# Two chunks' projections interleaved by kind, input weights loaded earlier, and a second weight pair prepared earlier, in an attention and gated-MLP kernel

## The chip, the cores and the metric

The kernel runs on one core of one Trainium2 chip. The metric is the device time of one execution in microseconds. Below, PE is TensorE (matmuls), DVE is VectorE, ACT is ScalarE, POOL is GpSimd and SP is SyncE; SP, ACT and POOL also issue DMA transfers.

## The reference

One sequence of S = 2048 tokens with D = 1024 goes through two blocks, each behind a layer norm and with a residual. All inputs are bfloat16.

```
A (sliding dilated attention, 32 heads of 32, window 8, step 2):
  q, k, v = layernorm(x) @ wqkv
  logits[s, w] = q[s] . k[s - 2w] / sqrt(32)     (masked where s - 2w < 0)
  o[s] = sum_w softmax(logits)[s, w] * v[s - 2w]
  h = x + o @ wo
B (gated MLP with a spatial product, Fh = 1792):
  z = gelu(layernorm(h) @ w_in);  z1 = z[:, :Fh];  z2 = layernorm(z[:, Fh:])
  g = w_sp @ z2 + b_sp[:, None]
  out = h + (z1 * g) @ w_out
```

## The kernel before

**First phase: chunks of 512 tokens.** The tokens are cut into four chunks (c = 0 to 3). For each chunk there is a chain: layer norm (`ln1`), a transpose by DMA into `xnT[c]` (SP), the three projections (`qkv`: q, k and v are kinds xi = 0, 1, 2, each four accumulators of 16 matmuls with 512 columns), their copies to `stg` on ACT and stores to `qkv_d` (SP), the loads of `qT`, `kT`, `vT` of the chunk from `qkv_d` (POOL; `ld` in `attention`), the attention itself, nearly all on DVE, the output projection with the residual (`head`), and the two halves of the input projection of block B: `b_z2` (L790, with win0 and win1 of `w_in`) and `b_z1` (L856, with win2 and win3). Chunk 0 keeps q, k and v on chip.

Inside `attention` the weights of the window are spread over the partitions: half of them through PE (L617), the other half through DRAM (`spread`: one store to `att_d`, four loads into `AB`, on SP). Two sums are gathered by accumulating DMAs on POOL (`av_y<-av_z` and `av_oT<-av_zz`, L655).

**The order of the first phase** is made by a planner, the class `Order`. Every step is added with an engine, an expected duration, its dependencies, a priority and the buffers that it takes and frees. `run()` then walks through time: on the engine that can start first, it takes the step of the lowest priority number among those that can start then (a step ahead by more than 0.5 in priority is also waited for, if it can start within 0.3 of the chosen step's duration). The functions are called in the order of the planned starts, and PE, ACT, DVE and POOL keep that order, whatever the real times are. The expected durations that matter here: four projection matmuls 0.8634, a load of `qT`, `kT` or `vT` 7.0, an `xnT` transpose 9.0, a spread 7.0, a load of win0 or win1 10.0. `order()` numbers the projection matmuls 6.001, 6.002 and so on in the order in which the calls of `qkv`, `b_z2` and `b_z1` add them; `head` has priorities near 4. There are three accumulators of two banks each and four `stg` buffers. `xnT` has two buffers.

`xnT[3]` waits for three things: the normalized rows, the last use of `xnT[1]`, and the load of `vT` of chunk 1 (`G["vload", 1]`), so that the transpose stays out of the way of the sums and loads.

The weights q and k lie in two buffers with tag `wA`, v and `wo` in two with tag `wB`. win0 and win1 take over the `wA` buffers when the last q and k matmul of chunk 3 is done. Loads of large weights are kept apart by hand: `behind_spread(i_, c)` makes a DMA wait until the spread of chunk c has landed; `G["win_i", k]` remembers a load behind which the next waits.

**Second phase: the spatial product.** After `o_.run()` everything is written in the order in which it is issued. `w_sp` is read transposed, in four column blocks `raw[0]` to `raw[3]` (`load_raw`, DMA transposes on SP), scaled by powers of two per row (`scale_raw`, with `rows`, which is the turned result of `row_scales`, read back from DRAM by `rows_in`), and combined into forms (`t_forms`). Blocks 0 and 1 are the first weight pair, 2 and 3 the second. For each pair there are NQ = 7 groups of 56 matmuls (L1060) that use `zs` (forms of z2 made on DVE by `z_form`, from `z2f`, which SP loads two groups ahead), and then eight output tiles with 28 matmuls each (L1161), which end in a DVE step (L1164) and a store. During the groups of the first pair the kernel also loads the rows of `w_sp` for the second half of the row scales (`load_wn`, on ACT's queue), sums them on ACT (`row_sum`), and loads `w_out` (POOL). During the output tiles of the first pair it scales and combines the second pair (`scale_raw(2)`, `scale_raw(3)`, `t_forms(1, ...)`, `z_form(NQ, ...)`).

`bank()` hands out the eight banks of PSUM in turn; the pool behind it starts at the bank at which the accumulators of the first phase started.

Of the kernel before, what the change touches and what calls it, by code (L numbers as in the profile page):

```python
# [22 lines left out]
P = 128  # L23
NT = S // P
CH = 512
# [107 lines left out]
def kernel(  # L133
# [251 lines left out]
    def load_win(k, t):  # L385
        c0, wd = win_specs[k]
        i_ = dma_w(t[:], win_view[:, :, c0:c0 + wd])
        if k == 0:
            behind_spread(i_, 1)
        elif k < 3:  # L390
            tc.add_manual_dep(i_.ins, G["win_i", k - 1].ins.name, wait_for, reason="one load of input weights after the other")
        G["win_i", k] = i_
        wins[k] = t

    o_ = Order({"PE": 22.4, "ACT": 23.6, "DVE": 15.4, "POOL": 12.0}, {"acc": 3, "L": 1, "prod": 1, "part": 2, "xn": 4})
# [52 lines left out]
        seq[0] += 1  # L448
        return 6.0 + seq[0] * 1e-3

    def qkv(c):
        for xi in range(0 if c else 1, 3):
            wv = wsb[xi][:].rearrange("p kt (m dl) -> p kt dl m", dl=DLO)
            for dp in range(DLO // 2):
                key = ("acc", "qkv", c, xi, dp)
                deps = [G.get(("xnT", c))]
                for j, k0 in PIECES:
                    def mm(j=j, k0=k0, dl=2 * dp + j, wv=wv, key=key):
                        if j == 0 and k0 == 0:
                            G[key] = new_acc()  # L460
                        for kt in range(k0, k0 + 4):
                            T.matmul(G[key][:, j, :].rearrange("p (a b) -> p a b", a=TPC), wv[:, kt, dl, :], xnT[c][:, :, kt, :],  # L462
                                     start=(kt == 0), stop=(kt == KT - 1))
                    last = add("PE", 0.8634, mm, deps, prio=order(), take="acc" if j == 0 and k0 == 0 else None)
                    deps = [(last, 0.0)]
                def ev(xi=xi, dp=dp, key=key):
                    if c == 0:
                        A.copy(att_in[0][xi][:, 2 * dp:2 * dp + 2, HALO:HALO + CH], G[key][:])  # L468
                        if dp == 3:
                            dma(qkv_d[xi][:, :, CH - HALO:CH], att_in[0][xi][:, :, CH:CH + HALO])  # L470
                    else:
                        stg = l1.tile([P, 2, CH], BF16, name="stg", tag="xn", bufs=4)
                        A.copy(stg[:], G[key][:])  # L473
                        dma(qkv_d[xi][:, 2 * dp:2 * dp + 2, c * CH:(c + 1) * CH], stg[:])
                G["ev", c, xi, dp] = add("ACT", 0.92, ev, [last], prio=2.0, free="acc", lat=0.15, take="xn" if c else None)
                if c:
                    dma_op(3.5, lambda: None, [G["ev", c, xi, dp]], free="xn")
            G["wdone", c, xi] = last
        G["qkvlast", c] = last
# [7 lines left out]
    def attention(c):  # L487
        if c == 0:
            d_q = add("DMA", 23.7, lambda: None)
            d_k, d_v = G["ev", 0, 1, 3], G["ev", 0, 2, 3]  # L490
        else:
            def ld(which):
                def f():
                    alloc_att_in(c, which)
                    lo = c * CH - (HALO if which else 0)
                    i_ = dma_w(att_in[c][which][:], qkv_d[which][:, :, lo:(c + 1) * CH])
                    if which == 1 and c == 1:
                        behind_spread(i_, c - 1)
                    if which == 2:
                        G["vload", c] = i_  # L500
                return f
            ev = [G["ev", c, xi, dp] for xi in range(3) for dp in range(4)]
            d_q = dma_op(7.0, ld(0), ev[0:4] + [G["qfree", c - 1]] )
            d_k = dma_op(7.0, ld(1), ev[4:8] + [G["qkdone", c - 1]] + ([(G["spread", 0], 0.3)] if c == 1 else []))
            d_v = dma_op(7.0, ld(2), ev[8:12] + [G["avdone", c - 1]])
            if c == 1:
                G["xnT", 3].deps.append((d_v, 0.1))
# [458 lines left out]
        V.tensor_tensor(t[:], x, y, op=op)  # L966


    qkv(0)
    dma_op(8.0, lambda: dma_w(wo_sb[:], A_wo.rearrange("(p dl) n -> p dl n", dl=DLO)), [G["wdone", 0, 2]])  # L970
    for c in range(1, NCH):
        ln1(c)
        qkv(c)

    def open_():
        load_win(2, wtile([P, KT, 1024], "win2", "wB"))
# [8 lines left out]
    G["win", 2] = dma_op(10.0, lambda: None, [G["open"]])  # L985
    G["win", 3] = dma_op(14.0, lambda: None, [G["open"]])

    wsp_sums()
    for c in range(NCH):
        attention(c)  # L990
        if c == 1:
            G["win", 0].deps.append((G["spread", 1], 0.1))
            G["win", 1].deps.append((G["win", 0], 0.1))
            G["open"].deps.append((G["win", 1], 0.1))
        if c < NCH - 1:
            head(c)
    for c in range(NCH - 1):
# [49 lines left out]

    p2 = ctx.enter_context(tc.tile_pool(name="p2", bufs=2))
    psq = ctx.enter_context(tc.tile_pool(name="psq", bufs=8, space=PSUM))

    def bank():
        return psq.tile([P, CH], FP32, name="bank", tag="bank", bufs=8)
# [23 lines left out]
    for pr in range(NCH // 2):  # L1076
# [5 lines left out]
        for i in range(NQ):  # L1082
# [21 lines left out]
            times(k3, zs[n, 4], b22, False)  # L1104
            nc.gpsimd.tensor_tensor(p7[:], p7[:], p5[:], op=ALU.add)
            if pr == 0:
                if 2 <= i <= 5:
                    for t in (TPP + 2 * i - 4, TPP + 2 * i - 3):
                        row_sum(t, 0)
                        row_sum(t, 1)  # L1110
                if 1 <= i <= 4:
                    for t in (TPP + 2 * i - 2, TPP + 2 * i - 1):
                        load_wn(t, p2, "wn", 2)
                if i == 4:
                    dma_w(wout_a[:], wout_view[:, 0:8, :])
                elif i == 5:
                    dma_w(wout_b[:], wout_view[:, 8:NF, :])
                elif i == 6:
                    row_scales(1)
            if i + 1 < NQ:  # L1120
                for m in (3, 1, 2, 4):
                    z_form(n + 1, m)
            if n + 2 < 2 * NQ:
                for hf in range(2):
                    load_z2f(n + 2, hf)
            if pr == 0 and i >= NQ - TPC:
                load_raw(2, i - NQ + TPC, i - NQ + TPC + 1)
            V.tensor_tensor(u[:], k2[:], p1[:], op=ALU.add)
            nc.gpsimd.tensor_tensor(p1[:], u[:], bt1, op=ALU.add)
            nc.gpsimd.tensor_tensor(u[:], u[:], bt2, op=ALU.add)  # L1130
# [11 lines left out]
        for il in range(2 * TPC):  # L1142
            t = 2 * pr * TPC + il
            if pr == 0 and il == 0:
                rps = psq.tile([P, 2 * CH], BF16, name="rpq", tag="bank", bufs=8)
                T.transpose(rps[0:TPP, 0:P], rsc16[:, TPP:NT], ident[:])
                A.copy(rscT[0:TPP, :], rps[0:TPP, 0:P])
                A.dma_start(rs_d[TPP:NT, :], rscT[0:TPP, :])
                load_raw(3, 0, 1)
                load_raw(3, 1, 2)  # L1150
                rows_in(1)
                bias_in(1, p2, "z1c", 2)
                load_raw(3, 2, 3)
                load_raw(3, 3, 4)
            if il + 3 < 2 * TPC:
                load_hr(t + 3)
            hr = hrs[t]

            def project(outs, lo, hi, f):
                wt, f0 = (wout_a, f) if f < 8 else (wout_b, f - 8)  # L1160
                T.matmul(outs, zg[:, f, il * P:(il + 1) * P], wt[:, f0, lo:hi], start=(f == 0), stop=(f == NF - 1))  # L1161

            def finish_(lo, hi, acc):
                V.scalar_tensor_tensor(hr[:, lo:hi], acc[:, 0:hi - lo], rv[:, t:t + 1], hr[:, lo:hi], op0=ALU.mult, op1=ALU.add)  # L1164

            if t < NT - 1:
                acc = [bank(), bank()]
                for f in range(NF):
                    for nh in range(2):
                        project(acc[nh][:], nh * CH, (nh + 1) * CH, f)  # L1170
                for nh in range(2):
                    finish_(nh * CH, (nh + 1) * CH, acc[nh])
                dma(out2d[t * P:(t + 1) * P, :], hr[:])
            else:
                for n, (lo, hi) in enumerate(LAST_COLS):
                    acc = bank()
                    for f in range(NF):
                        project(acc[:, 0:hi - lo], lo, hi, f)
                    finish_(lo, hi, acc)
                    (A.dma_start if n % 2 else dma)(out2d[t * P:(t + 1) * P, lo:hi], hr[:, lo:hi])  # L1180
            if pr == 0:
                if il == 1:
                    scale_raw(2, 0)
                    scale_raw(2, HK)
                elif il == 3:
                    scale_raw(3, 0)
                    scale_raw(3, HK)
                elif il == 4:
                    t_forms(1, 0)
                    t_forms(1, 3)  # L1190
                elif il == 5:
                    t_forms(1, 1)
                    t_forms(1, 2)
                elif il == 6:
                    for m in (3, 1, 2, 4):
                        z_form(NQ, m)
                    bias_rows(1)
# [32 lines left out]
```

## Time and profile before

| | us |
|---|---|
| median of 3 runs (lowest to highest) | 707.87 (707.87 to 708.66) |
| the profiled execution | 711.23 |
| span of its profile | 709.2 |
| PE busy | 695.8 |
| DVE busy | 508.8 |
| ACT busy | 276.6 |
| POOL busy | 120.5 |

The span runs from the first to the last instruction of the profiled execution; its time has 2.0 us more around it. Times in rows of the trace are microseconds from the start of the span. A row of the timeline has start, duration, engine, line, operation, output and inputs, count, and in brackets how long the engine stood before it and who released it. "SPq", "ACTq" and "POOLq" are the queues in which the engines issue DMAs; the landing of a DMA is told apart from its issue. The first phase ends at about 437 us; the groups of the first weight pair run until about 523, its output tiles until about 575, the second pair's until the end.

### The profile page before, as it was taken

What the parts mean: (1) busy time and instruction counts of PE and PEld (TensorE: products, weight loads), DVE (VectorE), ACT (ScalarE), POOL (GpSimd) and SP (SyncE); (2) the same over time, 40 slices, a digit from 0 to 9 for tenths busy, and PEclk for the clock granted to TensorE, in tenths of its full rate; (3) what the DMA queues carried; (4) which work ended last, traced back from release to release, by engine and by line L of the source; (5) the groups of instructions that cost most, each with busy time, mean ns of one, the idle gap of its engine ahead of it and who ended that gap; (6) DMA issues with size and microseconds to landing.
All of it is one profiled execution on the core that took longest, in us unless ns stands there. A gap on an engine that the chain in (4) does not pass through costs nothing.

```text
span 709.2 us, 8835 instructions
## 1 busy us (share of the span) xinstructions
PE 695.8 (98%) x3427; PEld 359.8 (51%) x3427; DVE 508.8 (72%) x614; ACT 276.6 (39%) x388; POOL 120.5 (17%) x113
## 2 busy tenths in 40 slices
PE   9999999999969999999999999999999999999998
PEld 7766665566624445444444544444444444444444
DVE  6899899999859989998895276556352995554322
ACT  4546652443316886664772552135400001111000
POOL 0100010011011101100120130434340013434000
PEclk9999999999989999999999999999999999999999
DMA  9978597577984369453673995678999636362121
GB/s 320 326 231 241 166 223 246 151 186 204 288 312 164 79 225 242 177 183 86 143 235 105 214 303 151 193 200 217 263 227 245 168 105 176 90 161 76 44 90 45
DMA packets 145290, 133.04 MB, mean 188 GB/s; under 512 B 68769, under 2 KB 117313, under 8 KB 145121
## 3 DMA queue, kind: packets, MB, share of 16 engines
q1 hardware_dynamic: 132784, 88.93, 45.3%
q0 software_dynamic: 7808, 32.97, 16.7%
q10 hardware_dynamic: 4656, 10.59, 4.6%
q8 instruction: 27, 0.44, 0.2%
q14 instruction: 15, 0.11, 0.1%
HBM read 75.24 MB, written 33.10 MB: 153 GB/s over the span
## 4 chain that ended last, share of the span: by engine, by line
PE 66%; DMA 2%; DVE 2%; issue 1%; SPq 0%; ACT 0%; DVEq 0%
PE bank L1060 24%; PE acc L856 14%; PE acc L790 13%; PE bank L1161 9%; PE acc L716 6%; DMA win<-in_B_w_in_dram 2%; DVE hr L1164 1%; DVE rawa L936 1%; DMA out_dram<-hr 0%; DMA brow<-in_B_b_sp_dram 0%; SPq L931 0%; DVE rawb L936 0%; DVE form L945 0%; DVE form L943 0%; PE L L555 0%
## 5 line engine op out<-in xcount | busy, mean ns | idle before, releaser
L790 PE MATMUL acc<-win,hnT 128*128 128x512 bf16 (+1 forms) x512 | 99.8, 357 | 6.7 <-DMA win<-in_B_w_in_dram 6.7
L856 PE MATMUL acc<-hnT,win 128*128 128x512 bf16 x448 | 98.0, 379 | 0.0
L790 PEld LDWEIGHTS <-hnT 128*128 128x128 bf16 x512 | 50.4, 99 | 55.5 <-DMA win<-in_B_w_in_dram 7.2
L525 DVE TENSOR_TENSOR prod<-qT,kT 128x4096 bf16<-128x4096 bf16 x32 | 72.8, 2286 | 2.1 <-ACT kT L468 1.3
L1060 PEld LDWEIGHTS <-zs 128*128 128x128 f16 x448 | 43.8, 98 | 54.4 <-DVE zs L966 1.8
L1161 PEld LDWEIGHTS <-zg 128*128 128x128 bf16 x462 | 44.6, 98 | 52.2 <-DVE zg L1138 0.2
L856 PEld LDWEIGHTS <-win 128*128 128x128 bf16 x448 | 43.7, 98 | 52.6 <-issue 0.7
L473 ACT CAST stg<-acc 128x1024 bf16<-128x1024 f32 x36 | 36.4, 1012 | 61.2 <-PE acc L462 55.8
L1096 ACT COPY p<-bank 128x512 f32<-128x512 f32 x14 | 8.2, 587 | 131.9 <-PE bank L1060 129.5
L1161 PE MATMUL bank<-wout_a,zg 128*128 128x512 bf16 (+2 forms) x264 | 58.2, 373 | 0.0
L462 PE MATMUL acc<-xnT,wk 128*128 128x512 bf16 x256 | 56.5, 379 | 0.0
L462 PE MATMUL acc<-xnT,wv 128*128 128x512 bf16 x256 | 56.1, 379 | 0.0
L716 PE MATMUL acc<-wo_sb,av_oT 128*128 128x512 bf16 x256 | 56.1, 379 | 0.0
L1060 PE MATMUL bank<-rawb,zs 128*128 128x512 f16 x224 | 52.9, 379 | 1.3 <-DVE zs L966 1.3
L1060 PE MATMUL bank<-rawa,z2f 128*128 128x512 f16 x224 | 52.9, 379 | 1.1 <-ACT z1s L862 1.1
L1060 PEld LDWEIGHTS <-z2f 128*128 128x128 bf16 x336 | 32.9, 98 | 40.9 <-issue 1.4
L1164 DVE SCALAR_TENSOR_TENSOR hr<-bank,rinv_w,hr 128x512 bf16<-128x512 f32 (+2 forms) x33 | 22.8, 730 | 42.4 <-PE bank L1161 37.3
L1060 PE MATMUL bank<-form,zs 128*128 128x512 f16 x224 | 50.6, 379 | 0.0
L462 PEld LDWEIGHTS <-wv 128*128 128x128 bf16 x256 | 36.6, 143 | 18.7 <-issue 0.2
L462 PEld LDWEIGHTS <-wk 128*128 128x128 bf16 x256 | 36.5, 143 | 18.8 <-issue 0.7
L1161 PE MATMUL bank<-wout_b,zg 128*128 128x512 bf16 (+2 forms) x198 | 44.4, 373 | 0.0
L862 ACT ACTIVATE z1s<-acc 128x1024 bf16<-128x1024 f32 x28 | 28.7, 1024 | 37.3 <-PE acc L856 33.0
(189 smaller groups left out, 946.3 us busy)
## 6 DMA issues: line engine op xcount, KB each, us to landing
z2f<-z_d SPq DMA_DIRECT2D x28, 512.0 KB, 5.5
qkv_d<-stg SPq DMA_DIRECT2D x36, 256.0 KB, 4.4
wn<-in_B_w_sp_dram ACTq DMA_DIRECT2D x16, 512.0 KB, 3.9
z1c<-z_d SPq DMA_DIRECT2D x14, 512.0 KB, 3.8
z_d<-z1s SPq DMA_DIRECT2D x21, 256.0 KB, 2.4
z_d<-u SPq DMA_DIRECT2D x12, 448.0 KB, 2.6
av_y<-av_z POOLq DMA_DIRECT2D x4, 1024.0 KB, 9.7
av_oT<-av_zz POOLq DMA_DIRECT2D x4, 1024.0 KB, 15.4
```

The source lines that it names most:

```text
L462: T.matmul(G[key][:, j, :].rearrange("p (a b) -> p a b", a=TPC), wv[:, kt, dl, :], xnT[c][:, :, kt, :], start=(kt == 0), stop=(kt == KT - 1))
L473: A.copy(stg[:], G[key][:])
L525: V.tensor_tensor(st["prod"][:], qT[:], kT[:, :, o:o + CH], op=ALU.mult)
L716: T.matmul(st["acc", il][:, nh, :], oTs[c][:, dl, il * P:(il + 1) * P], wo_sb[:, dl, nh * CH:(nh + 1) * CH], start=(dl == 0), stop=(dl == ...
L790: T.matmul(accf[:, n0:n1], hnTs[c][:, il, kt, :], wins[hf][:, kt, n0:n1], start=(kt == 0), stop=(kt == KT - 1))
L856: T.matmul(G["accy", c, fp][:, j, :].rearrange("p (a b) -> p a b", a=TPC), wt[:, kt, f0 * P:(f0 + 1) * P], hnTs[c][:, :, kt, :], start=(kt ...
L862: A.activation(z1s[:], G["accy", c, fp][:], ACTF.Gelu_apprx_tanh)
L936: V.tensor_tensor(raw[c][:, ks, :].bitcast(FP16), raw[c][:, ks, :], rows, op=ALU.mult)
L1060: T.matmul(dst[:], wts[:, k, :], mov[:, k, :], start=(first and k == 0), stop=(k == HK - 1), skip_group_check=not first)
L1096: A.copy(p1[:], k1[:])
L1161: T.matmul(outs, zg[:, f, il * P:(il + 1) * P], wt[:, f0, lo:hi], start=(f == 0), stop=(f == NF - 1))
L1164: V.scalar_tensor_tensor(hr[:, lo:hi], acc[:, 0:hi - lo], rv[:, t:t + 1], hr[:, lo:hi], op0=ALU.mult, op1=ALU.add)
```

## The change

First phase: the calls that add the projections are in another order. Chunk 0 and 1 are as before, then the layer norms of chunks 2 and 3 are added, then q of chunk 2, q of chunk 3, k of 2, k of 3, v of 2, v of 3. win0 no longer waits for the spread of chunk 1. The load of `kT` of chunk 2 now waits for that spread, as the load of `kT` of chunk 1 did for the spread of chunk 0 and still does. win1 waits for that `kT` load instead of for win0.

Second phase: six banks are allocated and not used, ahead of the first group. The loads and sums of the `w_sp` rows come one group earlier, the row scales with their turn through PE and DRAM one group earlier (from the first output tile into group 5), `load_raw(2)` two groups earlier, `load_raw(3)` in one call instead of four, and scaling, combining and the first `z_form` of the second pair one output tile earlier.

```
     def load_win(k, t):
         c0, wd = win_specs[k]
         i_ = dma_w(t[:], win_view[:, :, c0:c0 + wd])
-        if k == 0:
-            behind_spread(i_, 1)
-        elif k < 3:
+        if k in (1, 2):
             tc.add_manual_dep(i_.ins, G["win_i", k - 1].ins.name, wait_for, reason="one of the large loads after the other")
-        G["win_i", k] = i_
+        if k:
+            G["win_i", k] = i_
...
-    def qkv(c):
-        for xi in range(0 if c else 1, 3):
+    def qkv(c, xs):
+        for xi in xs:
...
-                    if which == 1 and c == 1:
+                    if which == 1 and c < 3:
                         behind_spread(i_, c - 1)
+                        G["win_i", 0] = i_
...
-            d_k = dma_op(7.0, ld(1), ev[4:8] + [G["qkdone", c - 1]] + ([(G["spread", 0], 0.3)] if c == 1 else []))
+            d_k = G["kload", c] = dma_op(7.0, ld(1), ev[4:8] + [G["qkdone", c - 1]] + ([(G["spread", c - 1], 0.3)] if c < 3 else []))
...
-    qkv(0)
+    qkv(0, (1, 2))
...
-    for c in range(1, NCH):
-        ln1(c)
-        qkv(c)
+    ln1(1)
+    qkv(1, (0, 1, 2))
+    ln1(2)
+    ln1(3)
+    for xi in range(3):
+        for c in (2, 3):
+            qkv(c, (xi,))
...
+    G["open"].deps.append((G["win", 1], 0.1))
     wsp_sums()
     for c in range(NCH):
         attention(c)
-        if c == 1:
-            G["win", 0].deps.append((G["spread", 1], 0.1))
-            G["win", 1].deps.append((G["win", 0], 0.1))
-            G["open"].deps.append((G["win", 1], 0.1))
+        if c == 2:
+            G["win", 1].deps.append((G["kload", c], 0.1))
...
+    for _ in range(6):
+        psq.tile([P, CH], FP32, name="bank", tag="bank", bufs=8)
...
             if pr == 0:
-                if 2 <= i <= 5:
-                    for t in (TPP + 2 * i - 4, TPP + 2 * i - 3):
+                if 1 <= i <= 4:
+                    for t in (TPP + 2 * i - 2, TPP + 2 * i - 1):
                         row_sum(t, 0)
                         row_sum(t, 1)
-                if 1 <= i <= 4:
-                    for t in (TPP + 2 * i - 2, TPP + 2 * i - 1):
+                if i <= 3:
+                    for t in (TPP + 2 * i, TPP + 2 * i + 1):
                         load_wn(t, p2, "wn", 2)
...
                 elif i == 5:
                     dma_w(wout_b[:], wout_view[:, 8:NF, :])
-                elif i == 6:
                     row_scales(1)
+                    rps = psq.tile([P, 2 * CH], BF16, name="rpq", tag="bank", bufs=8)
+                    T.transpose(rps[0:TPP, 0:P], rsc16[:, TPP:NT], ident[:])
+                    A.copy(rscT[0:TPP, :], rps[0:TPP, 0:P])
+                    A.dma_start(rs_d[TPP:NT, :], rscT[0:TPP, :])
...
-            if pr == 0 and i >= NQ - TPC:
-                load_raw(2, i - NQ + TPC, i - NQ + TPC + 1)
+            if pr == 0 and 1 <= i <= TPC:
+                load_raw(2, i - 1, i)
+            elif n == 5:
+                rows_in(1)
...
             if pr == 0 and il == 0:
-                rps = psq.tile([P, 2 * CH], BF16, name="rpq", tag="bank", bufs=8)
-                T.transpose(rps[0:TPP, 0:P], rsc16[:, TPP:NT], ident[:])
-                A.copy(rscT[0:TPP, :], rps[0:TPP, 0:P])
-                A.dma_start(rs_d[TPP:NT, :], rscT[0:TPP, :])
-                load_raw(3, 0, 1)
-                load_raw(3, 1, 2)
-                rows_in(1)
+                load_raw(3)
                 bias_in(1, p2, "z1c", 2)
-                load_raw(3, 2, 3)
-                load_raw(3, 3, 4)
...
-                if il == 1:
+                if il == 0:
                     scale_raw(2, 0)
                     scale_raw(2, HK)
-                elif il == 3:
+                elif il == 2:
                     scale_raw(3, 0)
                     scale_raw(3, HK)
-                elif il == 4:
+                elif il == 3:
                     t_forms(1, 0)
                     t_forms(1, 3)
-                elif il == 5:
+                elif il == 4:
                     t_forms(1, 1)
                     t_forms(1, 2)
-                elif il == 6:
+                elif il == 5:
                     for m in (3, 1, 2, 4):
                         z_form(NQ, m)
                     bias_rows(1)
```

More of the change, by code (lines that the diff above doesn't have):

```diff
@@ L387, in load_win @@
         i_ = dma_w(t[:], win_view[:, :, c0:c0 + wd])
-        if k == 0:
-            behind_spread(i_, 1)
-        elif k < 3:
-            tc.add_manual_dep(i_.ins, G["win_i", k - 1].ins.name, wait_for, reason="one load of input weights after the other")
-        G["win_i", k] = i_
+        if k in (1, 2):
+            tc.add_manual_dep(i_.ins, G["win_i", k - 1].ins.name, wait_for, reason="one of the large loads after the other")
+        if k:
+            G["win_i", k] = i_
         wins[k] = t
```

## The prediction

> **What bounds the kernel now.** I read the page's busy times first, then who TensorE (PE) waited for, then its clock around the longest wait, and then single rows of the queues that lead to that wait.
>
> ```profile
> PE 695.8 (98%) x3427; PEld 359.8 (51%) x3427; DVE 508.8 (72%) x614; ACT 276.6 (39%) x388; POOL 120.5 (17%) x113
> ```
>
> ```profile
> PE acc L790 <- DMA win<-in_B_w_in_dram: 6.7, 1, 6.7
> PE bank L1060 <- DVE zs L966: 1.3, 1, 1.3
> PE wps L226 <- DVE eps_t L229: 1.2, 1, 1.2
> PE bank L1060 <- ACT z1s L862: 1.1, 1, 1.1
> ```
>
> PE is busy for 98% of the span and waits for somebody four times in all. So a microsecond in which PE stands is a microsecond of the kernel, and nothing else counts unless it makes PE stand. The change can win at most three of these four waits and what hangs on them.
>
> The longest wait costs more than its 6.7 us. The rows of the windows (PE busy, PEld, DVE, ACT, POOL, then the granted clock) and of PE's timeline show it:
>
> ```profile
> 195.00:198.00 3.00, 0.02 (x1) 0.00 (x0) 1.44 (x1) 1.11 (x2) 0.00 (x0) 1.00 1.06 412
> 198.00:201.00 3.00, 0.00 (x0) 0.00 (x0) 3.00 (x3) 0.00 (x0) 0.00 (x0) 0.54 0.90 353
> 201.00:204.00 3.00, 2.28 (x7) 1.04 (x8) 2.26 (x2) 0.00 (x0) 1.77 (x3) 0.50 0.19 34
> 204.00:207.00 3.00, 3.00 (x14) 1.49 (x13) 0.00 (x0) 0.00 (x0) 0.86 (x1) 0.82 0.90 303
> ```
>
> ```profile
> 115.98 13.98 PE L716 MATMUL acc<-wo_sb,av_oT 128*128 128x512 bf16 x64
> 129.79 5.34 PE L462 MATMUL acc<-xnT,wk 128*128 128x512 bf16 x24
> ...
> 191.40 3.62 PE L790 MATMUL acc<-win,hnT 128*128 128x512 bf16 x16
> 201.72 3.76 PE L790 MATMUL acc<-win,hnT 128*128 128x512 bf16 x12 [6.70 <-DMA win<-in_B_w_in_dram]
> 205.32 13.98 PE L716 MATMUL acc<-wo_sb,av_oT 128*128 128x512 bf16 x64
> ```
>
> 64 matmuls of 512 columns start 13.81 us apart (115.98 to 129.79), 0.216 us each. The 12 after the wait are six pairs of 512 and 256 columns, so 6 x 1.5 x 0.216 = 1.94 us; they took 205.32 - 201.72 = 3.60. The clock column says why: 0.54 in 198 to 201 means half speed from about 198.2, some 3.2 us after PE fell idle, and 0.82 in 204 to 207 means full speed again from about 205.1. The wait therefore cost 6.70 + 1.66 = 8.36 us.
>
> **The change part by part: the first input weights.** The wait at 201.72 is for the second input weight block, win1. These are the POOL rows that lead to it, and the times from issue to landing:
>
> ```profile
> 90.54 1.26 POOL L655 DMA_DIRECT2D av_y<-av_z  x1 [17.60 <-PE acc L462]
> 91.81 0.93 POOL L496 DMA_DIRECT2D kT<-qkv_d  x1
> 94.65 1.20 POOL L655 DMA_DIRECT2D av_oT<-av_zz  x1 [1.92 <-DMA qkv_d<-stg]
> ...
> 171.18 1.24 POOL L655 DMA_DIRECT2D av_y<-av_z  x1 [16.06 <-PE acc L462]
> 172.32 1.04 POOL L387 DMA_DIRECT2D win<-in_B_w_in_dram  x1
> 175.25 1.19 POOL L655 DMA_DIRECT2D av_oT<-av_zz  x1 [1.89 <-DVE av_zz L638]
> 190.95 0.93 POOL L387 DMA_DIRECT2D win<-in_B_w_in_dram  x1 [14.52 <-DMA win<-in_B_w_in_dram]
> ```
>
> ```profile
> win<-in_B_w_in_dram POOLq DMA_DIRECT2D x1, 2048.0 KB, 18.1
> ```
>
> ```profile
> win<-in_B_w_in_dram POOLq DMA_DIRECT2D x1, 1536.0 KB, 10.7
> ```
>
> ```profile
> av_oT<-av_zz POOLq DMA_DIRECT2D x1, 1024.0 KB, 21.2
> ```
>
> win0 is issued at 172.32 and lands 18.1 us later, at 190.4; win1 waits for that (issue 190.95) and lands at 201.65, when PE starts again. The gather into av_oT, issued between them, lands at 196.45: the queue works in order, first the 2 MB, then the gather, then win1, which ends 5.2 us after the gather.
>
> The change takes win0 out of this stretch. It now needs only the last use of the q weights, and q of chunk 3 is moved forward. win0 then goes out near 147 (worked out below), over 40 us before PE needs it; qT of chunk 2, behind it on POOL, is needed only by DVE's products after chunk 1, some 40 us later too. What now stands in win0's place is kT of chunk 2, held until the spread of chunk 1 has landed, and win1 behind kT. Chunk 0 shows this very sequence: gather, kT behind the spread, second gather, at 90.54, 91.81 and 94.65.
>
> ```profile
> kT<-qkv_d POOLq DMA_DIRECT2D x1, 1056.0 KB, 12.7
> ```
>
> ```profile
> av_oT<-av_zz POOLq DMA_DIRECT2D x1, 1024.0 KB, 15.8
> ```
>
> From the first gathers (171.18 against 90.54) the two stretches lie 80.6 apart; 1.1 comes on top, as the next paragraph finds. So kT goes out at 91.8 + 81.7 = 173.5 and lands at 186.2; win1 goes out then. The gather lands at 94.65 + 15.8 + 81.7 = 192.2. With win1's 5.2 us behind the gather it is there at 197.4; where the rings overlap, as win1 is now ready long before the gather ends, a little sooner: I take 197.2. PE needs it after 16 matmuls of the first block, 191.40 + 1.1 + 3.45 = 195.95. That leaves a wait of 1.2 us, and its ends are 0 (kT as quick as the gather allows) and about 5 (kT as slow as win0's 18.1 us: win1 out at 191.6, landing 10.7 later at 202.3, and 6 if nothing overlaps). I take 1.2 because chunk 0 has the same three transfers. The Trainium skill, "DMA: Bandwidth & Descriptors", section "Anatomy of one DMA", has such a transfer cost about 2.0 us plus its bytes over 436 GB/s, an estimate of 5.6 us for win1, and by that alone the wait would be 0 and the sum 1.2 better. The trace's 10.7 us disagrees, because the queue was not empty, and the measurement decides.
>
> The gather, at 192.2 instead of 196.45, also lets DVE's last addition of chunk 1 come sooner; the output projection of chunk 1, which PE reaches after that wait and the 1.94 us of the twelve matmuls, at about 199, finds its input ready. DVE's next two products then end close to PE's first output rows, so DVE stays tied to PE as before: I cost this at nothing, at most 0.5.
>
> **q of chunk 3 moved forward.** It reads xnT of chunk 3, until now not needed before v of chunk 2 was done. The SP queue, where the transpose has its place:
>
> ```profile
> 124.77 4.98 SPq L439 DMA_TRANSPOSE xnT<-xns  x1
> 129.84 2.33 SPq L724 DMA_DIRECT2D h_d<-hb  x2
> 132.80 10.68 SPq L474 DMA_DIRECT2D qkv_d<-stg  x4
> ```
>
> ```profile
> xnT<-xns SPq DMA_TRANSPOSE x1, 8.7
> ```
>
> xnT lands at 133.47. The planner doesn't use that time but its own: xnT is due 7.0 + 9.0 + 0.2 = 16.2 us after the output projection of chunk 0 could start. That started at 115.98, and not at the piece before (115.12) plus the 0.26 that the planner looks ahead, so it was possible between 115.38 and 116.24, and xnT is due between 131.6 and 132.4. Until then the planner has only k of chunk 2, as before. Pieces of four matmuls (0.863 us) follow the projection's end at 129.79; the third ends at 132.38, and there q of chunk 3 is put. So "interleaved by kind" becomes: q of 2, most of k of 2, the projection, a bit of k, q of 3, the rest. PE stands from 132.4 to 133.5: 1.1 us, with ends 0 and 2.0 (one piece later or sooner). Everything PE does until 191 moves by it, the spread of chunk 1 too; that is the 1.1 above. q of 3 ends at 133.5 + 13.8 = 147.3, win0's issue. The other reordered matmuls and copies are as many and as long as before: nothing.
>
> **Six unused banks.** The 1.1 us wait is the first bank of the weight stage, which the last activation still reads. The allocation is shifted to the two banks that the attention left, so the first two products write elsewhere; the shared one comes third, two products of 8 x 0.216 = 1.7 us later, which is more than the 1.1 us waited. All 1.1 goes.
>
> **The second weight pair.**
>
> ```profile
> 548.58 4.50 DVE L936 TENSOR_TENSOR rawa<-rawa,rows 128x4096 f16<-128x4096 bf16 x2 [11.64 <-DMA brow<-in_B_b_sp_dram]
> ...
> 574.24 1.28 DVE L966 TENSOR_TENSOR zs<-z2f 128x1024 f16<-128x1024 bf16 x2
> ```
>
> The 1.3 us wait is at 575 for zs, the end of a DVE chain that began late: its first scaling stood 11.6 us for rows that came behind transposes on SP. The change moves transposes two groups earlier, row scales and their transpose one group, and every DVE step one output tile earlier (28 matmuls, 28 x 0.216 = 6.0 us). The chain gains far more than 1.3, so all of it goes. The PE transpose and its copy are moved, not added; row_scales, six tiny DVE steps, now lie ahead of a DVE wait of 6.9 us (next row). The moved transposes share SP with z2f loads:
>
> ```profile
> 509.51 0.69 DVE L966 TENSOR_TENSOR zs<-z2f 128x1024 f16<-128x1024 bf16 x1 [6.92 <-DMA z2f<-z_d]
> ```
>
> ```profile
> 512.85 1.89 PE L1060 MATMUL bank<-rawb,zs 128*128 128x512 f16 x8
> ```
>
> ```profile
> z2f<-z_d SPq DMA_DIRECT2D x2, 512.0 KB, 12.6
> ```
>
> ```profile
> z2f<-z_d SPq DMA_DIRECT2D x2, 512.0 KB, 6.4
> ```
>
> In the worst group (12.6 us to landing, beside wout) the form is made at 510.2 and used at 512.85: 2.65 us to spare. The group before it had a transpose and row-sum loads beside it, the mix that groups 1 to 3 now have, and landed in 6.4. So nothing is lost; the cover is that 2.65 us, and beyond it each microsecond costs one.
>
> **The sum.** -8.36 + 1.1 + 1.2 - 1.1 - 1.3 = -8.46 us. The profiled execution took 711.23 us, with a span of 709.2 and 2.0 around it; it would take 702.8, with a span of about 700.8. The median of the three runs is 707.87, 3.4 below the profiled execution; the waits are taken to be the same there, so 699.4.
>
> **The rivals.** *The second block stays late.* If kT lands as slowly as win0 did, PE waits about 5 us; past about 3.2 us the clock goes to half too, 1.7 more: 5.5 above my sum, 704.9. For it: the queue is full in this stretch; against it: chunk 0's 12.7. The Trainium skill, "TensorE: Matmul & The Clock Gate", Part 1, gives a free-running window of about 3.4 us; by it a wait of 3 us may or may not pay, and 198.2 less 195.0 in the trace agrees.
>
> *The late transpose (slower).* xnT of chunk 3 is now on the path. If SP issues it not at 124.77 but behind later stores, PE stands for every microsecond of that. Issued at 132.2, behind the next h stores, it would land at 140.9: 8.5 us and 1.7 of clock, 9.1 more than in my sum, 708.5, no change. That is the point of decision; behind the stores that follow, at 143.5, another 11.3 later, it would be about 720. Against it: nothing ahead of it on SP has moved.
>
> *z2f behind transposes (slower).* Groups 1 to 4 would each have to lose over 2.1 us, so z2f would have to land after 12.6 + 2.65 + 2.1 = 17.4 us instead of 6.4 to 12.6; at 18.5 the four lose 13 us, 712.
>
> *The order does not come out as said.* If win1 lands no sooner than before, only the two short waits go: 707.87 - 2.4 = 705.5.
>
> **How the numbers follow.** The forecast gets 0.70, the late block 0.12, the unchanged order 0.05, the late transpose 0.07, z2f 0.04, others 0.02. The predicted time is the forecast's 699.4. Its own range goes from 697.1 (both new waits at 0) to about 701.5. The range asked for reaches from 696.8 into the late block, to 704.0. A measurement of this kernel tells about 0.2% (1.4 us) from no change: faster 0.88, same 0.04 (parts of the two slower rivals near 708), slower 0.08.
>
> **What would show it.** PE's waits should have a new row of about 1 us for xnT at L462 near 132, one of 0 to 3 for win at L790 near 196, and none at L1060 for z1s or zs; the clock should stay 1.00 from 195 to 207. POOL should issue a win near 147, kT near 173.5, the second win near 186. I am wrong if PE waits over 3 us at either place, if the clock falls, or if L1060 waits for zs inside the first seven groups.

## The result, and the profile after

| | before | after | ratio (95% interval) |
|---|---|---|---|
| median of 6 runs each, us | 707.88 (707.73 to 708.66) | 703.73 (702.85 to 705.22) | 0.994 (0.9927 to 0.9953) |
| again, later, 29 and 6 runs | 708.21 | 704.78 (703.38 to 705.74) | 0.9948 (0.9934 to 0.9963) |
| profiled execution (span) | 711.23 (709.2) | 703.75 (702.0) | |

The kernel became faster by 4.15 us, in the direction forecast, but by half of the 8.46 us. 703.73 lies 0.3 inside the upper end of the stated range (704.0) and outside the forecast's own range (697.1 to 701.5). One of the 29 runs of before took 718.29 us at a clock of 0.990 and is left out of the ratio. The spans of the two profiles lie 7.2 us apart, so already the pair of profiles and the pair of medians tell different things. First who PE waits for, in the profile after (in total, times, longest; the rows for `eps_t` and `xn` lie in the first 16 us):

```profile
PE acc L790 <- DMA win<-in_B_w_in_dram: 2.6, 1, 2.6
PE wps L226 <- DVE eps_t L229: 1.2, 1, 1.2
PE bank L1066 <- ACT z1s L862: 1.1, 1, 1.1
PE tpt L299 <- DVE xn L288: 0.5, 1, 0.5
```

The wait for win1 went from 6.7 to 2.6, the one for zs is gone, the one for the last activation has not moved, and there is none for xnT. PE's timeline and the clock (the column before the last two) around win1:

```profile
129.54 2.75 PE L461 MATMUL acc<-xnT,wk 128*128 128x512 bf16 x12
132.13 13.98 PE L461 MATMUL acc<-xnT,wq 128*128 128x512 bf16 x64
...
191.15 3.62 PE L790 MATMUL acc<-win,hnT 128*128 128x512 bf16 x16
197.38 2.12 PE L790 MATMUL acc<-win,hnT 128*128 128x512 bf16 x12 [2.62 <-DMA win<-in_B_w_in_dram]
199.34 13.98 PE L716 MATMUL acc<-wo_sb,av_oT 128*128 128x512 bf16 x64
```

```profile
195.00:198.00 3.00, 0.62 (x4) 0.38 (x5) 3.00 (x3) 0.92 (x2) 0.12 (x1) 1.00 1.04 380
198.00:201.00 3.00, 3.00 (x18) 1.60 (x17) 1.79 (x1) 0.00 (x0) 2.52 (x3) 1.00 0.60 167
```

q of chunk 3 comes after exactly three more pieces of k, as worked out, and without a wait. The twelve matmuls behind win1 take 199.34 - 197.38 = 1.96 us, full speed. The two spans differ by 6.70 + 1.66 - 2.62 (win1 and clock) + 1.3 (zs) + 0.2 (PE is that much ahead before the change acts: the projection starts at 115.72 instead of 115.98) = 7.2. POOL's queue, and the times from issue to landing of kT, the second gather and win1:

```profile
146.41 0.93 POOL L387 DMA_DIRECT2D win<-in_B_w_in_dram  x1 [8.96 <-PE acc L461]
153.05 0.89 POOL L495 DMA_DIRECT2D qT<-qkv_d  x1 [5.71 <-DVE prod L525]
170.93 1.22 POOL L655 DMA_DIRECT2D av_y<-av_z  x1 [16.99 <-PE acc L461]
172.04 0.95 POOL L495 DMA_DIRECT2D kT<-qkv_d  x1
175.00 1.19 POOL L655 DMA_DIRECT2D av_oT<-av_zz  x1 [2.01 <-DVE av_zz L638]
185.54 0.93 POOL L387 DMA_DIRECT2D win<-in_B_w_in_dram  x1 [9.36 <-DMA kT<-qkv_d]
```

```profile
kT<-qkv_d POOLq DMA_DIRECT2D x1, 1056.0 KB, 12.9
```

```profile
av_oT<-av_zz POOLq DMA_DIRECT2D x1, 1024.0 KB, 16.8
```

```profile
win<-in_B_w_in_dram POOLq DMA_DIRECT2D x1, 1536.0 KB, 11.8
```

win0 is out at 146.4. kT lands at 184.9, and win1 follows it. The gather lands at 191.8 and win1 at 197.34, 5.5 us behind it: win1 is still last in a queue that works in order.

### The profile page after: what moved, and what is told of

Same layout as the page of the kernel before. It is cut to its first block, busy times and chain, and to the rows that moved or that the text cites. A ratio compares the mean times of both kernels' runs of the same rounds, so it can differ in the third digit from the quotient of the medians.

```text
span 702.0 us, 8824 instructions
## 1 busy us (share of the span) xinstructions
PE 693.4 (99%) x3427; PEld 359.1 (51%) x3427; DVE 508.4 (72%) x614; ACT 276.5 (39%) x388; POOL 120.7 (17%) x113
## 4 chain that ended last, share of the span: by engine, by line
PE 71%; DMA 2%; ACT 0%; DVE 0%; issue 0%
PE bank L1066 24%; PE acc L856 14%; PE bank L1164 14%; PE acc L790 13%; PE acc L716 6%; DMA win<-in_B_w_in_dram 2%; PE L L555 0%; ACT z1s L862 0%; PE pb L617 0%; DVE hr L1167 0%; PE rpq L1126 0%; PE rps L907 0%; PE pba L617 0%
## 5 line engine op out<-in xcount | busy, mean ns | idle before, releaser
L790 PE MATMUL acc<-win,hnT 128*128 128x512 bf16 (+1 forms) x512 | 98.2, 352 | 2.6 <-DMA win<-in_B_w_in_dram 2.6
```

The source lines that it names most:

```text
L790: T.matmul(accf[:, n0:n1], hnTs[c][:, il, kt, :], wins[hf][:, kt, n0:n1], start=(kt == 0), stop=(kt == KT - 1))
```

## The experiments

**Where the 8.4 us of before come from in a usual execution.** The kernel before, unchanged.

> The kernel before, unchanged, to see how its executions differ. Theory A (the wait for the second input weight block is always about as long as in the profile shown): executions near 707.9 have the same 6.7 us wait and 0.995 clock as the profile of 711.2, and the 3.4 us between them lie elsewhere. Theory B (that wait varies): executions near 707.9 have spans near 706 and, where a profile falls on one, a wait of 3 to 5 us at L790 and a clock nearer to 1.000, the rest of the rows being the same within a few tenths.

Measured: 708.69 us (707.26 to 712.14, 12 runs), ratio 0.9998 (0.9978 to 1.0019). Its profile, of an execution of 709.83 us (span 707.7), with the windows in the same columns as above:

```profile
PE acc L790 <- DMA win<-in_B_w_in_dram: 5.8, 1, 5.8
PE wps L226 <- DVE eps_t L229: 1.2, 1, 1.2
PE bank L1060 <- ACT z1s L862: 1.1, 1, 1.1
PE tpt L299 <- DVE xn L288: 0.6, 1, 0.6
```

```profile
198.00:201.00 3.00, 0.42 (x2) 0.14 (x3) 3.00 (x2) 0.00 (x0) 0.00 (x0) 0.72 0.87 313
201.00:204.00 3.00, 3.00 (x11) 1.50 (x10) 1.11 (x1) 0.00 (x0) 2.63 (x3) 0.50 0.44 97
204.00:207.00 3.00, 3.00 (x11) 1.18 (x10) 0.00 (x0) 0.00 (x0) 0.00 (x0) 0.65 1.02 406
```

Neither theory is quite right. The wait is a little shorter, 5.8, and the clock falls later (half speed from 199.3 to 206.1), so that 5.5 us of it lie on working matmuls and cost 2.8: together 8.6, no less than in the first profile. What is missing is the zs wait: this execution has no such row. The executions of the unchanged kernel differ by the clock too: with a mean clock of 0.997 or 0.998 they mostly take 707.3 to 708.4, with 0.995 mostly 708.4 to 710.4. This profile is of the second group, and none was taken of the first, in which the median of the result (707.88) lies; what the wait costs there is not shown.

**One half of the change alone.** The first phase alone (its diff without the hunks from the six banks on), and the second phase alone (those hunks without the rest):

```
first half alone:   range(6) banks, rows, transposes and scaling of the second pair as before
second half alone:  load_win, qkv(c, xs), behind_spread for kT of chunk 2 as before
```

> Only the first-phase half of the change (order of q, k, v of chunks 2 and 3, win0 early, kT of chunk 2 behind the spread, win1 behind kT). Theory A: 8.4 us of wait and clock become about 2.6 us of wait, so 707.9 - 5.7 = 702.2. Theory B: the wait was worth only 5 us in a usual execution, so 707.9 - 2.5 = 705.4. Both: no wait for xnT near 132, the zs wait of 1.3 us at the second pair stays.

> Only the second-phase half of the change (six unused banks, second weight pair sooner). Both theories of the first phase: no row for zs among PE's waits, 1.3 us gained, 706.6; the 1.1 us wait for the last activation stays although the banks are shifted, since it stayed in the profile after; if the shift did work without the first half, 705.5.

Measured: first phase alone 704.64 (703.10 to 705.58, 7 runs), ratio 0.9928 (0.99 to 0.9956); second phase alone 708.56 (707.68 to 709.39, 12 runs), ratio 0.9987 (0.997 to 1.0005), not told from nothing, where 1.3 us had been expected. The first half brings the gain, and its time lies between what the two theories expected. In its profile (703.1 span, clock 0.997) the wait is even shorter than in the profile after, and yet it costs more:

```profile
PE acc L790 <- DMA win<-in_B_w_in_dram: 2.0, 1, 2.0
```

```profile
195.00:198.00 3.00, 1.00 (x6) 0.59 (x7) 3.00 (x3) 1.11 (x2) 0.50 (x1) 0.97 1.05 387
198.00:201.00 3.00, 3.00 (x11) 1.38 (x10) 1.98 (x1) 0.00 (x0) 2.13 (x3) 0.50 0.80 233
201.00:204.00 3.00, 3.00 (x15) 1.33 (x14) 0.00 (x0) 0.00 (x0) 0.00 (x0) 0.96 1.02 406
```

After a wait of 2.0 us the clock goes to half from about 197.8 to 201.2, while PE works: 3.4 us at half speed, 1.7 us lost. In the profile after, a wait of 2.6 us cost no clock.

**The six banks.** The changed kernel without them:

```
-    for _ in range(6):
-        psq.tile([P, CH], FP32, name="bank", tag="bank", bufs=8)
```

> The changed kernel without the six unused banks. If the first product of the weight stage waits for the whole older pool of accumulators, whichever bank it takes: the same 1.1 us wait at the start of the weight stage and 703.7, no difference. If the banks bring something elsewhere (a bank freed later further on): a new wait of PE in the groups, 0.3 us or more slower.

Measured: 704.31 (703.05 to 705.65, 8 runs), 0.9924 (0.9897 to 0.9951) of before; its 1.1 us wait for the last activation is the same, at the same place. The banks change nothing that these runs can tell: if the six tiles move the first products to other banks, as the allocation says, the wait does not depend on which bank is written first. The wait for win1 is 2.3 us in this profile, and the clock falls to half here too, from about 196.7 to 200.2.

**The clock, again.** The changed kernel, unchanged, on a chip with the next three variants.

> The changed kernel, unchanged, for its executions on one chip beside the variants. Theory C (after a wait of 2 to 3 us it depends on the execution whether the clock falls to half for about 3.4 us, which costs 1.7): two groups of executions, near 703.4 with clock 1.000 and near 705.2 with 0.997 to 0.998. Theory D (a wait under about 3.2 us never costs clock): one group near 703.7, clock 1.000 throughout.

Measured: 703.38, 703.39 and 704.02 us with a clock of 1.000, and 705.54, 705.71 and 705.74 with 0.997 or 0.998. Two groups 2 us apart, as theory C says; the profile is of the second group:

```profile
195.00:198.00 3.00, 0.33 (x2) 0.22 (x3) 3.00 (x3) 1.11 (x2) 0.00 (x0) 0.99 1.05 388
198.00:201.00 3.00, 3.00 (x11) 1.37 (x10) 2.00 (x1) 0.00 (x0) 2.63 (x3) 0.50 0.60 156
201.00:204.00 3.00, 3.00 (x15) 1.46 (x14) 0.00 (x0) 0.00 (x0) 0.00 (x0) 0.94 1.00 401
```

It has a wait of 2.7 us and the clock at half from 197.9 to 201.4. So the wait that is left costs 2.6, or 4.4, from one execution to the next.

**win1 in place of kT.** kT of chunk 2 not held behind the spread, win1 behind the spread, the rest as changed.

```
-        if k in (1, 2):
+        if k == 1:
+            behind_spread(i_, 1)
+        elif k == 2:
...
-                    if which == 1 and c < 3:
+                    if which == 1 and c == 1:
```

> The changed kernel with kT of chunk 2 loaded as before (no wait for the spread of chunk 1) and win1 in its place, behind that spread. Theory E (the 2.6 us that PE still waits for win1 are bytes ahead of it in POOL's queue: gather, kT, gather): win1 lands near 188, no wait at L790, clock 1.000 in every execution, one group near 701.0, which is 2.3 under the better group of the changed kernel. Rival F (the load of kT, moved to 154, gets in the way of the spread and delays DVE): the wait moves to the window products L555 or L617 or the projection L716, 703 to 705. The gather lands near 194, so DVE may be up to 0.8 us later.

> The same as the variant with kT early, but without the second-phase half of the change. With no wait and no clock change left in the first phase this shows the second half by itself: the 1.3 us wait for zs comes back, 1.3 us slower than the variant with both halves. Rival: the second half is worth nothing or costs (other transfers in the groups): the same time within 0.5 us.

> The variant with kT early, and the last pair of z1 columns computed in two accumulators, each with its own activation of 512 columns instead of one of 1024. The first product of the weight stage waits for the last activation whichever bank it takes; an activation half as long should cut that wait from 1.1 to about 0.7 us, 0.4 us faster. If the wait does not depend on the activation's length: no difference.

Measured: 708.11 (707.56 to 709.81, 11 runs), ratio 1.0002 (0.9994 to 1.0011): the whole gain is gone. Without the second half 708.54, with the split activation 708.67, both at 1.0003. Theory E's variant failed by rival F, and harder than F said. In PE's waits and DVE's timeline of the variant with kT early:

```profile
PE acc L717 <- DVE av_oT L650: 4.7, 1, 4.7
```

```profile
180.39 2.29 DVE L642 TENSOR_TENSOR av_b<-vT,AB 128x4096 bf16<-128x4096 bf16 x1 [5.88 <-DMA AB<-att_d]
```

and its SP queue and POOL queue:

```profile
164.61 0.43 SPq L603 DMA_DIRECT2D att_d<-attn  x1
171.41 4.23 SPq L605 DMA_DIRECT2D AB<-att_d  x4
```

```profile
163.50 0.88 POOL L497 DMA_DIRECT2D kT<-qkv_d  x1 [9.74 <-DMA qkv_d<-stg]
```

kT does not go out at 154 as in the kernel before:

```profile
154.23 0.89 POOL L496 DMA_DIRECT2D kT<-qkv_d  x1
```

The stores of k that it reads are issued from 149.7 on, beside the load of win0 that the new order brings here, and those of 150 to 152 take long to land:

```profile
qkv_d<-stg SPq DMA_DIRECT2D x2, 256.0 KB, 10.7
```

So kT is issued at 163.5, 1.1 us ahead of the spread's store. The store, in this variant and in the profile after:

```profile
att_d<-attn SPq DMA_DIRECT2D x1, 128.0 KB, 6.7
```

```profile
att_d<-attn SPq DMA_DIRECT2D x1, 128.0 KB, 2.1
```

The store took 6.7 us to land instead of 2.1. The four loads into AB, which come behind it, now lie beside the first gather (issued at 170.76) and took 7.3 us (their median) instead of 2.6. DVE stood 5.9 us, PE 4.7, and the clock fell (0.995 or 0.998 in all eleven executions). win1 went out only at 180.9, after all this, and PE did not wait for it; so it is kT, and not win1, that got in the way. The Trainium skill, "DMA: Bandwidth & Descriptors", section "Queues, rings and completion order", has each DMA engine serve its queues in turn, packet by packet; that agrees with a 128 KB store on one queue that becomes three times as slow (6.7 us instead of 2.1) beside 1 MB on another. So the change's wait of kT for the spread is not a detail: with k finished later, kT needs it. The second expectation failed: without the second half there is no row for zs, and the time is 0.4 us longer, not 1.3. The third is met in its row, 0.7 instead of 1.1 for the last activation, but not in the time (708.67), which varies by more than that with the clock.

**win1 needed later.** Instead of moving loads, this moves PE's products in `b_z2` of chunk 0: the four against win0 first, then the four against win1 (before: alternating).

```
-        for il in range(TPC):
-            evs = []
-            for hf in range(2):
...
+        halves = [(il, hf) for il in range(TPC) for hf in range(2)]
+        if c == 0:
+            halves.sort(key=lambda x: x[1])
+        for il, hf in halves:
...
```

> The changed kernel, with the four products of chunk 0 against win0 put ahead of the four against win1 (before: alternating), so that PE needs win1 some 24 us later. Theory E (win1 comes last in POOL's queue, and its place there is all that PE waits for): no wait for win, clock 1.000 in every execution, one narrow group at 703.4 - 2.6 = 700.8. Rival G (PE then waits for the next thing that the queue brings, the gather that the projection of chunk 1 needs): a wait at L716 of 1 to 2 us, 702 or more.

> The same with the last pair of z1 columns in two accumulators with an activation of 512 columns each. The row of PE's waits for the last activation goes from 1.1 to 0.7 us as in the earlier split, 0.4 us faster than the variant with win0's products first, 700.4.

> The variant with win0's products first, without the second-phase half of the change. Theory H (the 1.3 us wait for zs belonged to the one long execution that was profiled first, since two later profiles of kernels with the old second phase don't show it): the same time within 0.4 us. Rival (the second half is worth its 1.3 us): 1.3 us slower.

Measured, on one chip beside 708.42 of before: 701.05 (700.74 to 701.34, 4 runs), ratio 0.9896 (0.9881 to 0.991); with the split activation 700.68 (700.27 to 700.80, 5 runs), 0.9889 (0.9875 to 0.9903), the lowest median of all and 0.4 below the first, as expected; without the second half 700.88 (700.79 to 703.72, 6 runs), 0.99 (0.9884 to 0.9915). The waits of the first, the last activation in the second, and the start of the projection of chunk 1 in the first:

```profile
PE wps L226 <- DVE eps_t L229: 1.2, 1, 1.2
PE bank L1071 <- ACT z1s L867: 1.1, 1, 1.1
PE acc L303 <- ACT xnT L300: 0.2, 1, 0.2
```

```profile
PE bank L1082 <- ACT z1s L870: 0.7, 1, 0.7
```

```profile
191.32 5.34 PE L793 MATMUL acc<-win,hnT 128*128 128x512 bf16 x23
196.50 13.98 PE L716 MATMUL acc<-wo_sb,av_oT 128*128 128x512 bf16 x63
```

win is gone from the waits, the clock is 1.000 in all fifteen executions, and without the two groups of the clock the times are narrow, but for one of 703.72, at full clock, that stays unexplained. Theory E stands, rival G falls. Theory H stands too: the second half makes no difference that these runs can tell (701.05 with it, 700.88 without).

**The same edit on the kernel before,** with nothing of the change.

> The kernel before, with nothing of the change, only the four products of chunk 0 against win0 put ahead of those against win1. If the order of PE's products were all, this would do as well as the same edit on the changed kernel, 700.8. If win0 in front of the second gather still costs (it landed at 195 to 196.5, so that the sums of chunk 1 end near 197 to 199 where the projection is now put at 196.3): a wait of 1 to 2.5 us at L716 for av_oT, with or without the clock, 702 to 704.5; and none for win at L790, unless win0 itself, which lands at 188 to 190.4, comes after 191.1.

Measured: 701.39 (701.33 to 702.22, 4 runs), ratio 0.9894 (0.9877 to 0.991), beside 708.92 of before.

```profile
PE acc L716 <- DVE av_oT L649: 0.3, 1, 0.3
```

```profile
172.11 1.18 POOL L387 DMA_DIRECT2D win<-in_B_w_in_dram  x1
```

```profile
win<-in_B_w_in_dram POOLq DMA_DIRECT2D x1, 2048.0 KB, 15.9
```

The order of PE's products is nearly all: win0 lands at 188.0, before PE asks for it at 191.3, and the second gather costs only 0.3 us. The 1 to 2.5 us that had been expected for the gather did not come.

## Why the prediction was right, and where its sizes were wrong

- **The number is inside the range partly by luck.** The forecast's own range ended at 701.5. The part above it had been added for the rival with the late second block, and that rival did not come.
- **The bound and the cause held.** PE was the bound, win1's place in POOL's queue the cause, and the first half of the change the gain.
- **The planner held.** q of chunk 3 came out after the projection and three pieces, win0 at 146.4 (147 forecast), kT at 172.0, win1 at 185.5.
- **The wait for xnT, 1.1: it did not come.** The prediction took 8.7 us from issue to landing, out of one profile. In all ten profiles of kernels with the new order it is 6.8:

```profile
xnT<-xns SPq DMA_TRANSPOSE x1, 6.8
```

  So xnT lands at 131.3, ahead of 132.1, and no wait is left. With the old order it was 8.7, 8.7, 8.6 and once 6.8 (the second half alone); what makes the difference was not traced.
- **The wait for win1, 1.2: it was 2.6.** The landing came out right (197.2 forecast, 197.34 measured), but by luck: without the 1.1 for xnT the gather went out 1.3 us sooner than forecast (175.0 instead of 176.3), and it then took 16.8 us instead of 15.8 to land, with win1 5.5 behind it instead of about 5.0. PE was there 1.2 us sooner (194.76 instead of 195.95), since xnT had not held it. The two terms together were 2.3 forecast and 2.6 measured: a wait taken from one place went to the next.
- **The clock after a short wait: a step that failed.** The sum let a wait under 3.2 us pass without a cost, although the prediction says elsewhere that a wait of 3 us may or may not pay. In four of the twelve executions of the changed kernel (one of the first six, 705.22, and three of the second six) the mean clock is 0.997 or 0.998, and they take about 2 us longer. In the three profiles with such a fall (the changed kernel again, the first half alone, the kernel without the banks) it cost 1.6 to 1.7 us, after waits of 2.7, 2.0 and 2.3. It did not make the measured 703.73, though: five of the first six executions have a clock of 1.000, and the median lies among them.
- **The banks, 1.1: failed.** It was argued from the layout that the first two products would find free banks. They wait all the same, 1.1 us, in the changed kernel with and without the banks; what shortens the wait is a shorter last activation. That the newer pool as a whole waits for the older one is the likely reason, but was only argued.
- **zs, 1.3: right in the profiles, not in the medians.** The chain did gain more than asked: in the profile after, zs is started at 555.05 for a weight stage that starts at 565.83.

```profile
555.05 1.28 DVE L966 TENSOR_TENSOR zs<-z2f 128x1024 f16<-128x1024 bf16 x2
```

```profile
565.83 1.89 PE L1066 MATMUL bank<-rawa,z2f 128*128 128x512 f16 x8
```

  But the wait that it took away stood in the one long execution that was profiled first. Five other profiles of kernels with the old second half have no such row. In the second profile of before it was close, with zs started 0.8 us ahead of the matmuls that read it:

```profile
572.67 1.28 DVE L966 TENSOR_TENSOR zs<-z2f 128x1024 f16<-128x1024 bf16 x2
```

```profile
573.48 1.89 PE L1060 MATMUL bank<-rawb,zs 128*128 128x512 f16 x8
```

- **The sum.** Forecast -8.46, measured -4.15 in the medians, so 4.3 are missing. About 1.0 of it is missing between the two profiled executions too, 711.23 and 703.75, where 702.8 was forecast: the banks brought nothing (1.1) and the two waits were longer (0.3), and about 0.4 went the other way, at the start and in the time around the span. The other 3.3 lie between the first profiled execution of before (711.23) and its median (707.88); the profile after has no such distance (703.75 and 703.73). So the step that cost most is "the waits are taken to be the same there". Of the 3.3, the zs wait is 1.3. The wait for win1 with its clock is hardly smaller in the other profiles with the old first half: 8.4 in the first, 5.8 + 2.8 in the second profile of before and 5.2 + 2.7 in the second half alone. But these are all executions at a clock of 0.995; those near 707.9 mostly have 0.997 or 0.998. That is one stretch of 3.4 us at half speed less, an estimate of up to 1.7 us from the rows above. No such execution was profiled, so this part stays open. An execution 3.4 us above the median was by itself a reason to doubt its waits.
- **The rivals.** "The second block stays late" did not come: PE waited 2.6 us, not 5, and in the profile after the clock did not fall. In the executions in which it falls, it does so after a shorter wait than that rival asked for. None of the slower ones came.

## What to carry to other kernels

When PE waits for a transfer that is last in a full queue, first ask whether PE has other work that it could do before it: moving the use of win1 back by some 24 us took one sorted list and gave more (0.9894 of before) than moving the loads forward (0.994). Moving a load also moves its neighbours, and a small transfer on the path next to a large one shows it first (2.1 to 6.7 us for a 128 KB store). And a profiled execution that is longer than the median holds waits that the median may not have: before a wait of a microsecond is worth a change, look for it in a second profile.

## What the runs showed of the hardware

The clock fell to half at waits of 2.0, 2.3 and 2.7 us, and not in the execution with one of 2.6; each time it stayed there for about 3.4 us, or for 6.8 us after the longer waits (the second profile of before: a wait of 5.8, half speed from 199.3 to 206.1). The Trainium skill, "TensorE: Matmul & The Clock Gate", Part 1, tells of a free-running window of about 3.4 us and of a fall after at least one idle window; the length agrees, but the traces here differ on the rest, for a wait of 2.0 us cannot fill a window. In the first half's profile the 3.4 us before the fall (194.4 to 197.8) held 2.0 us of rest and 1.4 of work. So in this kernel a wait of 2 us or more has to be priced with a chance of another 1.7; the waits of 0.3 and 1.1 us left the clock at 1.00.
